# Attention, soft mixture and a tanh layer on one core: moving M's steps, two joins, one square and the linear part's last steps

## The chip, the cores and the metric

The kernel runs on one core of one Trainium2 chip. The metric is the device time of one execution in microseconds (us); the profile shows one execution as a hardware profiler recorded it. The engines in it are TensorE (PE for matmuls, PEld for weight loads), VectorE (DVE), ScalarE (ACT), GpSimd (POOL) and the queue that issues the DMAs (SP).

## What is computed

Three layers follow one another on 3072 tokens of 512 numbers. The first two (a linear attention with decay, then a mixture of experts with soft routing) end about halfway through the span and the change does not touch them. The third is where the change lies:

```python
def _moe2_ref(x, w_in, w_out):          # x 3072x512, w_in 512x2048, w_out 2048x512
    h = x @ w_in
    g = h - np.tanh(h)
    return (g @ w_out).astype(np.float32)
```

The input x of this layer is itself a product of a 3072x32 gate c and a 32x512 table (the mixture's output, `so` in the kernel), so h = c (so w_in). The kernel never forms x: it builds M = so w_in (32x2048) and works on c M.

## The kernel before

**Chunks.** The third layer is a walk over 96 chunks, numbered n = 0 to 95. A chunk is one of six column groups of 512 tokens (c) with one of sixteen blocks of 128 hidden columns (f). `TURNS` lists the order as (c, first f, last f): (0,0-2), (1,0-2), (2,0-2), (3,0-4), (4,0-8), (5,0-12), and then the remaining blocks of each c. So chunks 0 and 1 belong to c 0, 2 and 3 to c 1, 4 and 5 to c 2, 6 to 9 to c 3, 10 to 17 to c 4, 18 to 29 to c 5, 30 to 39 to c 0, 40 to 53 to c 1, and so on.

**What a chunk does.** `d_of(n)` is one matmul into one of three PSUM banks taken in turn (L805), so the matmul of chunk n has to wait until chunk n-3 has been read. `s_of(n)` squares it on ACT (L809); for the chunks in `POOL_R` ACT also writes a copy e with a bias (L812). `r_of(n)` multiplies the two into r, on DVE (L823), or on GpSimd for the chunks in `POOL_R` = 13, 16, 21, 26, 29, 34, 37 (L821). `r` is called the rest below. `product` is the second matmul (L830), four per chunk, one for each quarter of the 512 tokens, into four PSUM banks that a stretch of one c shares. When a stretch ends, `keep` copies the four sums to SBUF (ACT, L836, in the first stretch of a c) or adds them to what is there (DVE, L838).

**The loop.** In step n of the loop the program issues d and s of chunk n+3 (`ahead`), the rest of chunk n+2, then decoding steps, then products of chunk n. In the last two chunks of a stretch the products of both are issued together at the last one, eight in a row. Last, `run(n)` issues what was put down for step n with `at(n, ...)`. The order in each engine's queue is the order of the program; it is written out by hand (`manual_schedule`), and each engine works through its own queue in order. The first chunk whose index is in `LATE` (8) has its d and s issued after the products of step 5 and ahead of that step's copies of sums.

**Decoding.** w_in and w_out come as 64-bit floats and are loaded raw in slabs wi0 to wi7 and wo0 to wo7. A slab is decoded in two halves, each a cast on GpSimd (`cast`, L117) followed by a join on DVE (`join`, L121), which takes two operands from SBUF. `DECODE_AT` names the step in which a slab's last join is issued; `LEAD` spreads the four operations over the steps k-3, k-2 (casts), k-1 and k (joins). The last join of a slab frees its buffer and lets SP load another slab. A decoded wo slab is rounded for the products by `round_wo`, the first half on ACT (L788), the second on GpSimd (L790).

**M.** Two wi slabs give a quarter m of M (four blocks f). `make_m` multiplies (L753) and copies the result to SBUF (L758); `turn_m` turns it (L778) and DVE copies the bias columns `mt` (L781); `put_m` spreads it (L765), ACT writes `ms` (L769) and DVE subtracts a remainder into 32 rows of it (L770). All d of the blocks of quarter m need that last instruction. For m 1 and 2 and 3 the three parts come 2, 3 and 4 steps behind the second slab's decoding (`DUE`); for the second half of quarter 0 they come in the steps `HALF` = 2, 3, 4. They share one PSUM bank (`MISC`), so each part waits for the copy out of the part before.

**The linear part.** A correction qc (128x512) is built late (`LINEAR` = 43, 47): `linear_2` multiplies in steps 43 to 46, `linear_3` in step 47 makes qr in PSUM (L891) and then qc: rows 0 to 63 by an ACT copy (L893), a rounded copy qh of the other rows by ACT (L894), and four DVE operations on 32 rows each in steps 48 to 51 (L897 to L902). The first four products with qc (L1066) stand in step 53, each behind the products of one token quarter.

Of the kernel before, what the change touches and what calls it, by code (L numbers as in the profile page):

```python
# [9 lines left out]
F32 = mybir.dt.float32  # L10
# [48 lines left out]
DECODE_AT = [0, 2, 4, 6, 10, 12, 14, 17, 21, 24, 26, 30, 33, 36]  # L59
LEAD = 3, 2, 1, 0  # L60
DUE = 2, 3, 4, 1
HALF = 2, 3, 4
LATE = 8,
LINEAR = 43, 47
CHECK = 57, 59, 63
# [7 lines left out]
def tile_main(ctx, tc, qkv, lam, phi, w1, w2, w_in, w_out, out):  # L73
# [501 lines left out]
    with pool("exp") as ep:  # L575
# [136 lines left out]
        def now(ops):  # L712
            for f in ops:
                f()
# [42 lines left out]
        rows = slice(js[0] * NS, (js[-1] + 1) * NS)  # L757
        (nc.vector.tensor_copy if half == 1 else nc.scalar.copy)(m_t[m][rows], mp_[rows])  # L758

    def put_m(m, half=None, bk=None):  # L760
        pp = bank(bk or MISC, [P, 4, P], "pp")
        js = range(4) if half is None else range(2 * half, 2 * half + 2)
        rows = slice(js[0] * NS, (js[-1] + 1) * NS)
        for j in js:
            nc.tensor.matmul(  # L765
                pp[:, j], put[rows, j], m_t[m][rows], start=True, stop=True, skip_group_check=True)
        pp = pp[:, js[0]:js[-1] + 1].rearrange("p j f -> p (j f)")
        sl = slice(m * 512 + js[0] * P, m * 512 + (js[-1] + 1) * P)
        nc.scalar.activation(out=ms[:, sl], in_=pp, func=AF.Copy)  # L769
        nc.vector.tensor_tensor(  # L770
            out=ms[64:96, sl], in0=pp[64:96], in1=ms[64:96, sl].bitcast(F32), op=ALU.subtract)
        placed.update(2 * m + j // 2 for j in js)

    def turn_m(m, half=None, bk=None):
        js = range(4) if half is None else range(2 * half, 2 * half + 2)
# [113 lines left out]
    def linear_3(qs):  # L889
        qr = bank(MISC, [P, DM], "qr")  # L890
        nc.tensor.matmul(qr, gsum, qs, start=True, stop=True)  # L891
        qh = lt_all[:, :DM]
        nc.scalar.activation(out=qc[:64], in_=qr[:64], func=AF.Copy)  # L893
        nc.scalar.activation(out=qh[64:].bitcast(F32R), in_=qr[64:], func=AF.Copy)  # L894
        ql = tmp("e", bufs=2)
        return [
            lambda: nc.vector.tensor_tensor(out=ql[96:], in0=qr[96:], in1=qh[96:], op=ALU.subtract),  # L897
            lambda: nc.vector.tensor_scalar(
                out=ql[96:], in0=ql[96:], scalar1=ends[96:, 1:2], scalar2=0.0, op0=ALU.mult, op1=ALU.add),
            lambda: nc.vector.scalar_tensor_tensor(  # L900
                out=qc[96:], in0=qh[96:], scalar=ends[96:, 0:1], in1=ql[96:], op0=ALU.mult, op1=ALU.add),
            lambda: nc.vector.tensor_tensor(  # L902
                out=qc[64:96], in0=qr[64:96], in1=qh[64:96], op=ALU.subtract),
        ]


# [65 lines left out]
        return z  # L972

    LA = 3
    due = {}

    def at(n, f):
        due.setdefault(n, []).append(f)

    def run(n):  # L980
        for f in due.pop(n, []):
            f()

# [18 lines left out]
    early[0]()  # L1002
    round_wo(0, 1)
    r_of(1)
    now(early[1:])

    def decoded(n, w, i):
        if w == "wi" and i == 1:
            at(HALF[0], lambda: make_m(0, 1))
            at(HALF[1], lambda: turn_m(0, 1))  # L1010
            at(HALF[2], lambda: put_m(0, 1))
        elif w == "wi" and i % 2:
            at(n + DUE[0], lambda: make_m(i // 2))
            at(n + DUE[1], lambda: turn_m(i // 2))
            at(n + DUE[2], lambda: put_m(i // 2))
            if i == NF // 2 - 1:
                at(LINEAR[0] - 3, linear_0)
                at(LINEAR[0] - 3, linear_1)
                at(LINEAR[0] - 2, linear_g)
                at(LINEAR[0] - 1, lambda: state.update(gt=linear_gt()))  # L1020
        elif w == "wo":
            for h in range(2):
                at(n + DUE[3] + h, lambda h=h: round_wo(i, h))
            if i == NF // 2 - 1:
                for j in range(4):
                    at(LINEAR[0] + j, lambda j=j: linear_2(state["gt"], j))
                at(LINEAR[1], lambda: state.update(linear=linear_3(state["qs"])))
                for j in range(4):
                    at(LINEAR[1] + 1 + j, lambda j=j: state["linear"][j]())
                at(CHECK[0], check_1)  # L1030
                at(CHECK[1], check_2)
                at(CHECK[2], lambda: state.update(flag=check_3()))

    for n in range(NN):
# [4 lines left out]
            ahead()  # L1039
        if n + LA - 1 < NN:  # L1040
            r_of(n + LA - 1)
        for slab, k in zip(parts, DECODE_AT):
            for h, lead in enumerate(LEAD):
                if k - lead == n and k:
                    parts[slab][h]()
            if k == n:
                decoded(n, *slab)
# [9 lines left out]
                product(*s, n, f == lo, False)  # L1057
        if last:

            for s in ops:  # L1060
                if hi - lo > 1 and n > 1:
                    product(*s, n - 1, f - 1 == lo, False)
                product(*s, n, f == lo, hi < NF)
                if hi == NF:
                    op, t, sl = s
                    nc.tensor.matmul(op, c4[:, c, t * P:(t + 1) * P], qc[:, sl], start=False, stop=True)  # L1066
            if n + LA in LATE:
                ahead()
            for s in ops:
                keep(c, *s, lo, hi)  # L1070
        run(n)
    assert not due, sorted(due)
    scheduled.close()


# [82 lines left out]
```

## Time and profile before

| | us |
|---|---|
| median of three runs | 311.65 (311.45 to 311.79) |
| the profiled execution's own time | 311.51 |
| its span, first to last instruction | 309.6 |

| engine | busy us | share of the span |
|---|---|---|
| PE | 294.8 | 95% |
| DVE | 181.3 | 59% |
| ACT | 134.3 | 43% |
| POOL | 115.2 | 37% |

TensorE was granted its full clock nearly throughout (mean 0.995). The third layer begins at about 155 us of the span. In the views below a row of the timeline gives start, duration, engine, line, operation, output and inputs, shapes, count, and in brackets how long the engine sat idle before it and what released it. A duration includes any time in which the instruction had begun and was held up inside the engine. Several instructions that follow one another directly are merged into one row with their count. The d matmuls of L805 stand in the order of the chunks, so the number of a chunk is found by counting them.

### The profile page before, as it was taken

How to read it: one execution, taken by the hardware profiler on the slowest of the kernel's cores; microseconds unless marked ns; L12 is line 12 of the kernel's file. 1: busy time of each engine (PE TensorE's matmuls, PEld its weight loads, DVE VectorE, ACT ScalarE, POOL GpSimd, SP SyncE). 2: the span in 40 equal slices, each digit the busy share in tenths (PEclk: the TensorE clock that was granted, in tenths of full speed). 3: DMA queues.
4: the chain of work that ended last, by engine and by line, in shares of the span. 5: the costliest groups of instructions: out<-in, count | busy, mean ns of one | idle time of the engine just before them, and what ended most of it. 6: DMA issues, size and time to landing. Idle time of an engine off the chain costs nothing.

```text
span 309.6 us, 7420 instructions
## 1 busy us (share of the span) xinstructions
PE 294.8 (95%) x2996; PEld 213.6 (69%) x2996; DVE 181.3 (59%) x330; ACT 134.3 (43%) x280; POOL 115.2 (37%) x167
## 2 busy tenths in 40 slices
PE   8999999999999999999989889999999899999992
PEld 7788787878878774445466567777655677787771
DVE  4844455544654244520269667696872877968783
ACT  1433343344333433232248669586633554454420
POOL 6366566765653104112276445686600001000000
PEclk9999999999999999999999999999999999999997
DMA  6999999999999999999988747562000030303154
GB/s 209 386 402 395 396 399 394 395 399 398 392 403 396 383 362 344 389 393 396 391 308 318 268 142 285 194 230 110 0 2 0 2 135 0 135 2 135 70 202 143
DMA packets 32679, 79.77 MB, mean 258 GB/s; under 512 B 3008, under 2 KB 3328, under 8 KB 32640
## 3 DMA queue, kind: packets, MB, share of 16 engines
q1 hardware_dynamic: 32512, 79.18, 68.5%
q8 instruction: 25, 0.41, 0.5%
q14 instruction: 14, 0.11, 0.1%
q0 software_dynamic: 128, 0.07, 0.1%
HBM read 72.94 MB, written 6.29 MB: 256 GB/s over the span
## 4 chain that ended last, share of the span: by engine, by line
PE 80%; DVE 8%; issue 4%; DMA 3%; ACT 2%; POOL 1%; DVEq 0%; ACTq 0%; POOLq 0%
PE ops L830 22%; PE sc L286 7%; PE xp L310 7%; PE dps L805 6%; PE op L610 5%; PE hp L586 5%; PE xnp L344 4%; PE xp L303 4%; DVE r L823 3%; PE up L319 3%; DMA qk<-in_qkv 3%; DVE part L838 2%; PE ltp L333 2%; PE ap L388 2%; PE wp L419 2%
## 5 line engine op out<-in xcount | busy, mean ns | idle before, releaser
L830 PE MATMUL ops<-wr,r 128*128 128x512 f32 (+1 forms) x388 | 109.0, 397 | 1.2 <-ACT part L836 0.9
L830 PEld LDWEIGHTS ops<-wr,r 128*128 128x128 f32 x388 | 72.3, 188 | 22.2 <-ACT part L836 3.1
L809 ACT ACTIVATE s<-dps 128x512 f32<-128x512 f32 x96 | 56.9, 603 | 54.1 <-PE dps L805 52.8
L823 DVE SCALAR_TENSOR_TENSOR r<-dps,mt,s 128x512 fp32r<-128x512 f32 x89 | 64.8, 746 | 20.2 <-ACT s L809 19.4
L805 PE MATMUL dps<-c,ms 128*128 128x512 f32 x96 | 39.5, 425 | 4.2 <-DVE r L823 2.3
L290 DVE TENSOR_TENSOR at<-sc,dtab 128x512 f32<-128x512 f32 x48 | 30.8, 683 | 15.1 <-PE sc L286 15.1
L265 POOL TENSOR_TENSOR kc<-k,dtab 128x512 f32<-128x512 f32 x20 | 21.2, 1058 | 26.6 <-PE up L319 23.6
L258 POOL TENSOR_TENSOR qs<-qk,ql 128x512 f32<-128x512 f32 x20 | 25.5, 1275 | 14.6 <-DMA qk<-in_qkv 14.5
L346 ACT COPY xn<-xnp 128x512 f32<-128x512 f32 x24 | 14.0, 585 | 38.9 <-PE xnp L344 38.9
L286 PE MATMUL sc<-qk 64*128 64x128 f32 x384 | 27.9, 285 | 1.4 <-DMA qk<-in_qkv 1.4
L805 PEld LDWEIGHTS dps<-c,ms 128*128 128x128 f32 x96 | 17.9, 188 | 15.6 <-DVE r L823 7.8
L310 PE MATMUL xp<-at,v 128*64 128x128 f32 x384 | 26.3, 279 | 0.0
L286 PEld LDWEIGHTS sc<-qk 64*128 64x128 f32 x384 | 23.3, 187 | 4.2 <-issue 1.9
L313 ACT COPY xt<-xp 128x256 f32<-128x256 f32 x48 | 17.9, 372 | 16.9 <-PE xp L310 16.4
L310 PEld LDWEIGHTS xp<-at,v 128*64 128x64 f32 x384 | 20.5, 136 | 4.1 <-issue 3.9
L325 DVE TENSOR_TENSOR st<-up,sd 128x256 f32<-128x256 f32 x16 | 6.8, 425 | 23.4 <-PE up L319 22.0
L117 POOL CAST top<-wi 128x512 f16<-128x512 bf16 x16 | 14.3, 907 | 13.7 <-DMA wi<-in_w_in 13.1
L838 DVE TENSOR_TENSOR part<-ops,part 128x512 f32<-128x512 f32 (+1 forms) x29 | 17.9, 665 | 0.9 <-PE ops L1066 0.9
L610 PE MATMUL op<-w,hz 128*32 128x512 f32 x128 | 16.5, 594 | 0.0
L117 POOL CAST top<-wo 128x512 f16<-128x512 bf16 x16 | 15.2, 978 | 2.3 <-DMA wo<-in_w_out 2.1
L121 DVE SCALAR_TENSOR_TENSOR wif<-wi,top 128x512 uint32<-128x512 uint32 x16 | 13.3, 842 | 4.2 <-POOL top L117 4.2
L344 PE MATMUL xnp<-cst,xt 128*128 128x128 f32 x96 | 15.7, 287 | 0.0
(185 smaller groups left out, 344.3 us busy)
## 6 DMA issues: line engine op xcount, KB each, us to landing
w<-in_w SPq DMA_DIRECT2D x64, 512.0 KB, 8.4
qk<-in_qkv SPq DMA_DIRECT2D x24, 512.0 KB, 8.4
wi<-in_w_in SPq DMA_DIRECT2D x16, 512.0 KB, 4.0
wo<-in_w_out SPq DMA_DIRECT2D x16, 512.0 KB, 4.2
v<-in_qkv SPq DMA_DIRECT2D x24, 256.0 KB, 8.5
out<-part SPq DMA_DIRECT2D x23, 256.0 KB, 2.2
k<-in_qkv SPq DMA_DIRECT2D x14, 256.0 KB, 8.0
out<-part SPq DMA_DIRECT2D x2, 128.0 KB, 3.5
```

Source lines behind the costliest of these rows:

```text
L117: nc.gpsimd.tensor_copy(out=every(top().bitcast(F16), 2, 1)[:, sl], in_=every(raw().bitcast(BF16)[:, 4:], 4, 0)[:, sl])
L258: nc.gpsimd.tensor_tensor(out=qs_t[u], in0=qk_t[u][:, 0], in1=ql, op=ALU.mult)
L286: nc.tensor.matmul(sc[h2][:, p], qk[sl, 1, p], qk[sl, 0, p], start=True, stop=True)
L290: nc.vector.tensor_tensor(out=by_head(at_t[u], h2), in0=sc[h2], in1=by_head(dtab, h2), op=ALU.mult)
L310: nc.tensor.matmul(at_head(p, h2), v[:, h * DH:(h + 1) * DH], at[:, h], start=c == 0 and p < 2, stop=True, skip_group_check=True)
L344: nc.tensor.transpose(xnp[:, p], xt[:, p // 2, p % 2], ident)
L610: nc.tensor.matmul(op[g * NS:(g + 1) * NS], hz_t[e % 3][:, q], w2_t[e, q // 4][:, g], start=e == 0 and q < 4, stop=e == NE - 1 and q >= 4, ...
L805: nc.tensor.matmul(d_t[n], ms[:, f * P:(f + 1) * P], c4[:, c], start=True, stop=True)
L809: nc.scalar.activation(out=s, in_=d_t[n], func=AF.Square, scale=math.sqrt(1.0 / 3))
L823: nc.vector.scalar_tensor_tensor(out=r_t[n], in0=d, scalar=mt[:, f, NS:], in1=s, op0=ALU.add, op1=ALU.mult)
L830: nc.tensor.matmul(op, r_t[n][:, t * P:(t + 1) * P], wr_t[f // 2][:, f % 2, sl], start=first, stop=last)
L838: nc.vector.tensor_tensor(out=pt, in0=op, in1=pt, op=ALU.add)
```

## The change

Eight things are moved or rewritten; the arithmetic is the same.

1. Joins of wi1 (two halves): they stood in front of the loop behind the rest of chunk 1; now the first stands behind the rest of chunk 2 (step 0) and the second behind the rest of chunk 3 (step 1).
2. The second half of M's quarter 0: `make_m(0, 1)` goes from the end of step 2 to the middle of step 3's eight products; `turn` and `put` stay in the steps 3 and 4.
3. The square of chunk 8 is issued behind the four copies of sums of step 5 (its d stays ahead of them).
4. Quarter 1 of M: make, turn and put go from the ends of the steps 8, 9, 10 to the end of 7, the middle of 9 and the end of 9; ACT's and DVE's parts of the put are split in two pieces of 256 columns.
5. Quarter 2: from steps 19, 20, 21 to 18, 19, 20.
6. Quarter 3: steps as before (32, 33, 34), but ACT's and DVE's part of the put is issued in step 35, behind the rest of chunk 37.
7. The linear part: in step 48 ACT copies 64 rows of qr to SBUF and GpSimd does five operations on 32 rows each; DVE's four are gone. ACT's copy to rows 0 to 63 of qc goes behind that, to step 49.
8. Helpers (`at_mid`, `at_r`) for work that is issued in the middle of a step's products or right behind its rest.

```diff
-HALF = 2, 3, 4
+HALF = 3, 3, 4
+SECOND = 7, 9, 9
+THIRD = 18, 19, 20
@@ def put_m(m, half=None, bk=None, pieces=1, later=None)
-        nc.scalar.activation(out=ms[:, sl], in_=pp, func=AF.Copy)
-        nc.vector.tensor_tensor(
-            out=ms[64:96, sl], in0=pp[64:96], in1=ms[64:96, sl].bitcast(F32), op=ALU.subtract)
+        def take(i):
+            src = pp[:, js[0] * P + i * n:js[0] * P + (i + 1) * n]
+            sl = slice(m * 512 + js[0] * P + i * n, m * 512 + js[0] * P + (i + 1) * n)
+            nc.scalar.activation(out=ms[:, sl], in_=src, func=AF.Copy)
+            return lambda: nc.vector.tensor_tensor(
+                out=ms[64:96, sl], in0=src[64:96], in1=ms[64:96, sl].bitcast(F32), op=ALU.subtract)
+        def place():
+            for rest in [take(i) for i in range(pieces)]:
+                rest()
+        if later is None:
+            place()
+        else:
+            at_r(later, place)
@@ def linear_3(qs)
-        nc.scalar.activation(out=qc[:64], in_=qr[:64], func=AF.Copy)
+        qf, ql = tmp("e", bufs=2), tmp("e", bufs=2)
+        tt = lambda out, in0, in1, op: nc.gpsimd.tensor_tensor(out=out, in0=in0, in1=in1, op=op)
+        end = lambda i: ends[96:, i:i + 1].to_broadcast([32, DM])
         nc.scalar.activation(out=qh[64:].bitcast(F32R), in_=qr[64:], func=AF.Copy)
+        def rest():
+            tt(qc[64:96], qf[64:96], qh[64:96], ALU.subtract)
+            tt(ql[96:], qf[96:], qh[96:], ALU.subtract)
+            tt(ql[96:], ql[96:], end(1), ALU.mult)
+            tt(qf[96:], qh[96:], end(0), ALU.mult)
+            tt(qc[96:], qf[96:], ql[96:], ALU.add)
         return [
-...
+            lambda: (nc.scalar.copy(qf[64:], qr[64:]), rest()),
+            lambda: nc.scalar.activation(out=qc[:64], in_=qr[:64], func=AF.Copy),
         ]
@@ main loop
-    now(early[1:])
+    cast_1, join_0, join_1, *early = early[1:]
+    now([cast_1] + early)
+    at_r(0, join_0)
+    at_r(1, join_1)
-            at(HALF[0], lambda: make_m(0, 1))
+            at_mid(HALF[0], lambda: make_m(0, 1))
+        elif w == "wi" and i == 3:
+            at(SECOND[0], lambda: make_m(1))
+            at_mid(SECOND[1], lambda: turn_m(1))
+            at(SECOND[2], lambda: put_m(1, pieces=2))
+        elif w == "wi" and i == 5:
+            at(THIRD[0], lambda: make_m(2))
+            at(THIRD[1], lambda: turn_m(2))
+            at(THIRD[2], lambda: put_m(2))
-            at(n + DUE[2], lambda: put_m(i // 2))
+            at(n + DUE[2], lambda: put_m(i // 2, later=n + DUE[2] + 1))
-                for j in range(4):
+                for j in range(2):
                     at(LINEAR[1] + 1 + j, lambda j=j: state["linear"][j]())
+        run(n, due_r)
-            for s in ops:
+            for i, s in enumerate(ops):
+                if i == 2:
+                    run(n, due_mid)
             if n + LA in LATE:
-                ahead()
+                d_of(n + LA)
             for s in ops:
                 keep(c, *s, lo, hi)
+            if n + LA in LATE:
+                s_of(n + LA)
```

## Rows read from the trace of the kernel before

**Rows 1.** PE's waits, 155 to 310 us: waiter, releaser, us in total, times, longest.
```profile
PE dps L805 <- DVE ms L770: 1.7, 2, 1.4
```
**Rows 2.** The chain that ended last: start, us, what.
```profile
189.57 1.91 PE ops L830 x7
...
250.32 0.93 PE ops L830 x4
```
**Rows 3.** Timeline, square of chunk 8, copies of step 5, products of chunk 6.
```profile
171.24 0.60 ACT L809 ACTIVATE s<-dps 128x512 f32<-128x512 f32 x1 [1.79 <-PE dps L805]
171.73 2.05 ACT L836 COPY part<-ops 128x512 f32<-128x512 f32 x4
...
172.36 1.97 PE L830 MATMUL ops<-wr,r 128*128 128x512 f32 x4 [0.93 <-ACT part L836]
```
**Rows 4.** Timeline, joins of wi1, d of chunk 5, DVE's copy in make_m(0, 1).
```profile
160.82 2.11 DVE L121 SCALAR_TENSOR_TENSOR wif<-wi,top 128x512 uint32<-128x512 uint32 x2
...
163.65 0.50 PE L805 MATMUL dps<-c,ms 128*128 128x512 f32 x1 [0.74 <-DVE r L823]
...
166.14 0.29 DVE L758 COPY lt_all<-mp__2509 64x128 f32<-64x128 f32 x1
```
**Rows 5.** Timeline, d of chunk 13, its e, d of chunk 14.
```profile
179.03 0.48 PE L805 MATMUL dps<-c,ms 128*128 128x512 f32 x1
...
180.09 0.74 ACT L812 ACTIVATE e<-dps,mt 128x512 f32<-128x512 f32 x1
...
182.74 0.50 PE L805 MATMUL dps<-c,ms 128*128 128x512 f32 x1 [1.41 <-DVE ms L770]
```
**Rows 6.** Timeline of POOL, rests of chunks 13 and 16, casts of wi4, rounding of wo3.
```profile
180.91 1.26 POOL L821 TENSOR_TENSOR r<-e,s 128x512 fp32r<-128x512 f32 x1 [6.02 <-ACT e L812]
182.12 1.92 POOL L117 CAST top<-wi 128x512 f16<-128x512 bf16 x2
...
186.92 1.35 POOL L821 TENSOR_TENSOR r<-e,s 128x512 fp32r<-128x512 f32 x1 [2.35 <-ACT e L812]
...
188.90 0.62 POOL L790 CAST wr<-wf 128x512 fp32r<-128x512 f32 x1
```
**Rows 7.** Timeline, joins that meet GpSimd's work.
```profile
201.27 2.39 DVE L121 SCALAR_TENSOR_TENSOR wf<-wo,top 128x512 uint32<-128x512 uint32 x2
...
201.81 1.30 POOL L821 TENSOR_TENSOR r<-e,s 128x512 fp32r<-128x512 f32 x1 [2.74 <-issue]
...
204.22 0.60 POOL L790 CAST wr<-wf 128x512 fp32r<-128x512 f32 x1
204.24 1.12 DVE L121 SCALAR_TENSOR_TENSOR wif<-wi,top 128x512 uint32<-128x512 uint32 x1
```
**Rows 8.** Timeline, d of chunk 38, put_m(3) on ACT and DVE, d of chunk 42.
```profile
216.93 0.48 PE L805 MATMUL dps<-c,ms 128*128 128x512 f32 x1
217.22 0.60 ACT L769 ACTIVATE ms<-pp 128x512 fp32r<-128x512 f32 x1 [0.58 <-PE pp L765]
...
217.85 0.69 DVE L770 TENSOR_TENSOR ms<-pp,ms 32x512 fp32r<-32x512 f32 x1 [1.73 <-ACT ms L769]
...
221.36 0.50 PE L805 MATMUL dps<-c,ms 128*128 128x512 f32 x1 [0.45 <-DVE r L823]
```
**Rows 9.** Timeline, linear part: qh, d of chunk 56, first product with qc, d of chunk 58.
```profile
240.01 0.59 ACT L894 ACTIVATE lt_all<-qr 64x512 fp32r<-64x512 f32 x1
...
245.04 0.50 PE L805 MATMUL dps<-c,ms 128*128 128x512 f32 x1 [0.79 <-DVE r L823]
...
245.85 0.47 PE L1066 MATMUL ops<-qc,c 128*128 128x512 f32 x1
...
249.93 0.39 PE L805 MATMUL dps<-c,ms 128*128 128x512 f32 x1
```
**Rows 10.** Groups of POOL instructions by form: count, busy us, mean ns, idle before.
```profile
L258 POOL TENSOR_TENSOR qs<-qk,ql 128x512 f32<-128x512 f32 x20 | 25.5, 1275 | 14.6 <-DMA qk<-in_qkv 14.5
L265 POOL TENSOR_TENSOR kc<-k,dtab 128x512 f32<-128x512 f32 x20 | 21.2, 1058 | 26.6 <-PE up L319 23.6 <-ACT k L253 2.7 <-POOL qs L258 0.3
...
L635 POOL COPY put<-cst 32x96 f32<-32x96 f32 x4 | 1.0, 256 | 0.0
```

More of the change, by code (lines that the diff above doesn't have):

```diff
@@ L758, in make_m, with put_m @@
         (nc.vector.tensor_copy if half == 1 else nc.scalar.copy)(m_t[m][rows], mp_[rows])
-    def put_m(m, half=None, bk=None):
+    def put_m(m, half=None, bk=None, pieces=1, later=None):
         pp = bank(bk or MISC, [P, 4, P], "pp")
@@ L766, in put_m @@
                 pp[:, j], put[rows, j], m_t[m][rows], start=True, stop=True, skip_group_check=True)
-        pp = pp[:, js[0]:js[-1] + 1].rearrange("p j f -> p (j f)")
-        sl = slice(m * 512 + js[0] * P, m * 512 + (js[-1] + 1) * P)
-        nc.scalar.activation(out=ms[:, sl], in_=pp, func=AF.Copy)
-        nc.vector.tensor_tensor(
-            out=ms[64:96, sl], in0=pp[64:96], in1=ms[64:96, sl].bitcast(F32), op=ALU.subtract)
-        placed.update(2 * m + j // 2 for j in js)
+        pp = pp.rearrange("p j f -> p (j f)")
+        n = len(js) * P // pieces
+        def take(i):
[7 more added lines that the diff above has]
+                rest()
+            placed.update(2 * m + j // 2 for j in js)
+        if later is None:
+            place()
+        else:
+            at_r(later, place)
     def turn_m(m, half=None, bk=None):
@@ L892, in linear_3 @@
         qh = lt_all[:, :DM]
-        nc.scalar.activation(out=qc[:64], in_=qr[:64], func=AF.Copy)
+        qf, ql = tmp("e", bufs=2), tmp("e", bufs=2)
+        tt = lambda out, in0, in1, op: nc.gpsimd.tensor_tensor(out=out, in0=in0, in1=in1, op=op)
+        end = lambda i: ends[96:, i:i + 1].to_broadcast([32, DM])
         nc.scalar.activation(out=qh[64:].bitcast(F32R), in_=qr[64:], func=AF.Copy)
-        ql = tmp("e", bufs=2)
-        return [
[L897 to L903, printed above, removed]
+        def rest():
[4 more added lines that the diff above has]
+            tt(qc[96:], qf[96:], ql[96:], ALU.add)
+        return [
+            lambda: (nc.scalar.copy(qf[64:], qr[64:]), rest()),
+            lambda: nc.scalar.activation(out=qc[:64], in_=qr[:64], func=AF.Copy),
         ]
@@ L974, in tile_main, with at_mid, at_r, run @@
     LA = 3
-    due = {}
+    due, due_mid, due_r = {}, {}, {}
     def at(n, f):
         due.setdefault(n, []).append(f)
-    def run(n):
+    def at_mid(n, f):
+        due_mid.setdefault(n, []).append(f)
+    def at_r(n, f):
+        due_r.setdefault(n, []).append(f)
+    def run(n, due=due):
         for f in due.pop(n, []):
@@ L1067, in tile_main @@
             if n + LA in LATE:
-                ahead()
+                d_of(n + LA)
             for s in ops:
                 keep(c, *s, lo, hi)
+            if n + LA in LATE:
+                s_of(n + LA)
         run(n)
-    assert not due, sorted(due)
+    assert not due and not due_mid and not due_r
     scheduled.close()
```

## The prediction

> **What bounds the kernel now.** I read the waits of PE first, then the chain that ended last, then the timeline around each place that the diff touches. All of them lie in the third layer, 155 to 310 us. PE is the bound there: a product takes 0.233 us (four in 0.93, [rows 2]), a chunk has five matmuls, and in most steps the next chunk starts 1.16 us after the last. So only the places where PE stands still count. The ones near the change are these. The d of chunk 5 waits 0.74 us for a rest that stands behind two joins [rows 4]. The products of chunk 6 wait 0.93 us for copies of sums [rows 3] and are then spread over 1.97 us. The d of chunk 14 waits 1.41 of the 1.7 us that PE loses to `ms` [rows 1, 5]; the other wait, that of chunk 26, is 0.25. At 189.57 a product waits for GpSimd's rounding of wo3, which ends at 189.52 [rows 2, 6]. The d of chunk 42 waits 0.45 us for DVE [rows 8], that of chunk 56 0.79 us [rows 9]. These sum to under 5 us, so no part of the change can bring much more, and each must be followed to what is late next.
>
> **The joins and M's quarter 0 (1, 2).** With the joins behind the rests of chunks 2 and 3, the d of chunk 5 no longer waits: 0.74 us off. But DVE's work up to its copy for make_m(0, 1) is the same, and DVE runs without a gap from 160.82 on. Before, that copy stands at 166.14 [rows 4]; now the rest of chunk 5 and a join of wi2 (0.7 and 0.9) stand ahead of it, so it ends at about 167.9 and turn_m, next on PE, waits for it. Before, turn ran at 167.4. The products of chunks 4 and 5 follow at 169.0 against 168.9. Gain of both: 0 (from -0.3 to 0.2).
>
> **The square behind the copies (3).** The square of chunk 8 begins at 171.24 because its d comes after eight products; the four copies queued behind it begin at 171.73, one each 0.49 us ((2.05-0.60)/3), and the products of chunk 6 keep that pace until 174.33 [rows 3]. Without the square the first copy can begin when its sum is whole, two products after 169.0, at 169.6, and the fourth at about 171.0. Chunk 6 then starts behind the d of chunk 9 at 171.4 and is done at 172.4: 1.9 us sooner. The square itself is 0.3 us later and so is the second join of wi3, which make_m(1) needs; at about 173.5 that costs PE 0.1. Gain 1.9 (1.5 to 2.1).
>
> **Quarter 1 a chunk sooner (4).** Make (1.0 us), turn (0.25) and put (0.9) now all stand ahead of the d of chunk 13. In sum PE reaches the d of chunk 14 with `ms` already written: 1.41 us more, so about 3.3 us at that point, 179.4 against 182.74. But chunk 13 gains only 0.9: its d goes from 179.03 to 178.1, since put and its wait on DVE's copy of mt stand ahead of it, and on ACT its square and its e stand behind the four copies of step 9 and the two pieces of the put. Its e then ends at 179.75 against 180.83 [rows 5].
>
> **What is late next: GpSimd.** That e releases GpSimd's queue: rest 13 (1.26), two casts of wi4 (1.92), rounding of wo2 (0.61), rest 16 (1.35), cast of wi5 (0.7), rounding of wo3 (0.62) [rows 6]. Before, GpSimd also sat idle 2.35 us in it, waiting for chunk 16's e, and the rounding that PE needs ended 8.6 us after rest 13 began. Now PE comes sooner and that idle time goes. Five joins of DVE (wo2's second, two of wo3, two of wi4) then fall between. [rows 7] show what a join costs that meets GpSimd: two joins took 2.39 us, the second ending 0.55 after the rest that began at 201.81 and took 1.30; a join at 204.24 took 1.12, ending 0.54 after the rounding of 204.22. So the two do not overlap: whichever began first is finished, the other then needs about 0.54. Without any meeting GpSimd's chain is 6.0 to 6.5 us, and the product that waits would come at about 186; with five joins in between (5 x 0.54 = 2.7) it is 8.5 to 8.9, and comes at 179.8 + 8.5 = 188.3 (rest 17 on DVE, which also needs those joins, comes at 187 to 188.7). The joins are queued back to back in just this stretch, so I take the serial value. Of 3.3 us, **1.2** are left at 189.57 (0.7 to 3.0). That is the gain of parts 1 to 4.
>
> **Quarter 2 (5).** The 0.25 us at chunk 26 goes. But DVE works without a gap from the instruction after that to about 212 us, and its copy of mt and its part of the put now stand ahead of rests 22 and 23, so it enters that stretch no sooner; PE then waits longer for rest 28 at 206. Gain 0 (-0.3 to 0.4).
>
> **Quarter 3 later (6).** On DVE the order does not change: rest 36, the subtraction, the first join of wo7, rest 38. DVE already sits idle 1.73 us in front of that subtraction, waiting for ACT [rows 8]. ACT's write of `ms` now goes behind a rounding of wo6 and the square of chunk 38, whose d ends at 217.41: square 217.43, write 217.92 to 218.52, subtraction at 218.55 against 217.85. So DVE is 0.70 later, and behind it without a gap stand two joins, rests 38 to 41 and four additions of sums, for which PE already waits at chunk 42 [rows 8] and again for the sums. Nothing covers it: **0.7 lost** (0 to 0.8).
>
> **Linear part (7).** ACT: qh 239.4 to 240.0 (0.59, [rows 9]), square of chunk 51, then the copy of qr, done at 241.1. DVE's four operations (0.70, 0.48, 0.75, 0.69) leave its queue, so rest 53 and the d of chunk 56 come without a wait: PE reaches the first product with qc at 244.8 instead of 245.85 [rows 9]. GpSimd needs five operations for qc. No row shows one on 32 partitions of 512; with 128 partitions, two operands cost 1.275 and one operand repeated 1.058 [rows 10]. That fewer partitions do not help is suggested by L635 (32x96 in 0.256, with 0.268 for L913's 128x96). So 3 x 1.275 + 2 x 1.058 = 5.94, and qc is whole at 247.1: PE stands still 2.3 us. From there to the d of chunk 58 are 15 matmuls, 3.5 us: 250.6 against 249.93 [rows 9], **0.7 lost**. The upper bound is five of 1.35 (rest 16, [rows 6]): 6.75, 1.5 lost. The lower is a cost that falls with the partitions: then qc is there before PE, and 1.7 us of waits of before (0.79, and DVE's lag behind it) go. DVE is free, but it wasn't what PE would wait for.
>
> The Trainium skill speaks against this part: GPSIMD Engine Reference, § 4.1 Engine selection, wants elementwise work on a tile on VectorE, since GpSimd is about twice as slow with two inputs. § 3.1 measures 4497 ns for 2048 columns; a quarter of it is 1.12 us as an estimate, five of them 5.6, and the loss would be 0.35 instead of 0.7. The rows agree on the direction (1.275 against DVE's 0.69 to 0.75).
>
> **Sum.** 1.2 + 0 - 0.7 - 0.7 = 0.2 lost on the profiled execution's 311.51, whose span is 309.6 with 1.9 around it; nothing outside the span changes. The median is 311.65, so I forecast **311.8**.
>
> **Rivals.** (a) Slower: the five GpSimd operations hold the first product with qc longer than I take. From 6.4 us on (1.28 each, or a start 0.5 later) the sum is over 0.6 lost; at 6.9 the product comes at 248.0, 1.6 lost instead of 0.7, and the time is 312.7. For it: the operations depend on one another, and nothing covers PE there. Against: rows of 1.06 for repeated operands. (b) Faster: joins and GpSimd's work meet less often than I let them, so that 2.6 of the 3.3 us survive: 310.3. For it: in the stretch of before, GpSimd's idle 2.35 us let the joins through; DVE may find other gaps. (c) Faster: GpSimd's operations on 32 partitions cost about what half the columns cost, 0.6 each, so qc is ready at 244.2 and 1.7 is gained, not 0.7 lost: 309.4. Against: L635. (d) Part 6 does not do what its place says, because DVE's first join of wo7 hides the later subtraction: 0.7 less, 311.1. Against: the join stands behind it in the queue.
>
> **Chances.** About 0.2% (0.6 us) is what a measurement of this kernel can tell from no change. Forecast 0.42, (a) 0.29, (b) 0.16, (c) 0.08, (d) 0.05. Faster by over 0.2%: (b) and (c), 0.24. Within: forecast and (d), 0.47. Slower: (a), 0.29. The range goes from a little under (b) to (a): 309.9 to 312.8, leaving out (c) and the far ends.
>
> **What would show it.** In the profile of the changed kernel: the four copies of step 5 begin before the square of chunk 8, and chunk 6's products end near 172.4 (part 3). The d of chunk 14 begins near 179.4 without a wait for DVE (part 4). The rounding of wo3 ends about 1.3 us sooner than 189.52, joins among GpSimd's rests last 1.1 us or more, and PE stands still at the products of chunks 16 and 17 (the chain). ACT's write of M's quarter 3 stands behind the square of chunk 38, DVE's subtraction 0.7 later against the d of chunk 38 (part 6). The first product with qc waits over 2 us for POOL (part 7). I am wrong if GpSimd's five operations take under 4 us, if the rounding of wo3 ends more than 2 us sooner, or if DVE catches up the 0.7 us before the sums of chunk 39.

## The result and the profile after

| | before | after |
|---|---|---|
| median, same comparison, us | 311.45 | 314.50 |
| ratio, 95% interval | | 1.0066 (1.0040 to 1.0092) |
| the profiled execution's own time, us | 311.51 | 314.61 |
| its span, us | 309.6 | 312.8 |
| PE busy, us | 294.8 | 296.8 |
| POOL busy, us | 115.2 | 122.5 |

The change makes the kernel slower, by 0.7% in the ratio of the comparison and by 1.0% in the two medians; 0.2 us, under 0.1%, was forecast, and the time lies above the range. The times of after spread from 312.35 to 316.23 us (disturbed executions, here 317.25 and 317.75, in e4 316.23 and in f1 314.32, are left out of spreads, means and ratios). They follow roughly the mean granted clock of each execution: 0.996 at 312.35, 0.994 at 312.67, 0.992 at 314.61, 0.986 at 315.57. That points at TensorE's clock before any line is read.

To find the place I divide the third layer at four instructions that all kernels have: M0 is the first matmul of the first `make_m`, and d14, d38, d44, d58 are the starts of the first matmuls of these chunks. All rows of this table come from the timeline of one profiled execution of each kernel. "e" to "h" are the experiments below. "Fall" says that the granted clock drops in that stretch from full speed to about half.

| kernel | M0 to d14 | d14 to d38 | d38 to d44 | d44 to d58 |
|---|---|---|---|---|
| before | 27.48 | 34.19 | 8.47 | 24.53 |
| after | 24.96 | 36.74 | 9.19 | 27.21, fall |
| e1, part 7 undone | 24.84 | 36.77 | 9.18 | 24.54 |
| e2, after with the wait filled | 25.97, fall | 36.74 | 9.19 | 25.79 |
| e3, parts 1 to 5 | 26.29, fall | 36.75 | 8.47 | 24.54 |
| e4, e3 with rests on DVE | 25.28 | 35.40 | 8.46 | 24.52 |
| f1, after with `linear_2` packed | 27.88, long fall | 36.74 | 9.20 | 22.78 |
| f2, parts 1 and 2 | 27.96 | 34.22 | 8.48 | 24.53 |
| f3, parts 3 to 5, rests on DVE | 24.56 | 35.47 | 8.46 | 24.54 |
| f4, f3 with packed part 7 | 24.39 | 35.47 | 8.47 | 22.79 |
| g1, after again | 23.88 | 36.78 | 9.19 | 25.78 |
| g2, e2 again | 26.32, fall | 36.75 | 9.20 | 25.79 |
| g3, part 7 alone | 27.46 | 34.22 | 8.47 | 27.32, fall |
| g4, before with rests on DVE | 27.43 | 34.15 | 8.46 | 24.52 |
| h1, after without parts 1, 2 | 24.76 | 36.75 | 9.18 | 27.22, fall |
| h2, h1 with the wait filled | 24.75 | 36.76 | 9.18 | 25.79 |
| h3, part 7 alone again | 27.41 | 34.19 | 8.48 | 27.20, fall |
| h4, part 7 alone, wait filled | 27.43 | 34.22 | 8.47 | 25.81 |

The first two rows carry the result: 2.52 us less to d14, 2.55 more to d38, then 0.72 and 2.68 more, 3.43 in all. The profiled executions differ by 3.10; the layers before and the end of the third account for the remaining 0.3.

**Where PE waits now.** PE's waits in the third layer of after: waiter, releaser, us in total, times, longest.
```profile
PE dps L820 <- DVE r L838: 3.7, 8, 1.1
PE ops L1108 <- POOL qc L909: 2.5, 1, 2.5
PE tp L793 <- DVE lt_all L760: 1.0, 1, 1.0
```
The wait for `ms` of [rows 1] is gone. In its place stand a wait for qc of 2.5 us, one of 1.0 behind DVE's copy in `make_m(0, 1)`, and more waits of a d for a rest on DVE.

**What became of the gain at d14.** Timeline of after: start, us, engine, line, operation, out and in, count, and in brackets the idle time before it and its releaser.
```profile
167.33 0.29 DVE L760 COPY lt_all<-mp__2521 64x128 f32<-64x128 f32 x1
167.67 0.43 PE L793 MATMUL tp<-tsel,lt_all 64*128 64x66 f32 x2 [1.01 <-DVE lt_all L760]
169.87 2.05 ACT L851 COPY part<-ops 128x512 f32<-128x512 f32 x4 [0.28 <-PE ops L845]
171.54 1.09 PE L845 MATMUL ops<-wr,r 128*128 128x512 f32 x4
171.78 1.77 ACT L824 ACTIVATE s<-dps 128x512 f32<-128x512 f32 x3
...
178.55 0.48 PE L820 MATMUL dps<-c,ms 128*128 128x512 f32 x1
180.00 0.51 PE L820 MATMUL dps<-c,ms 128*128 128x512 f32 x1
180.63 1.29 POOL L836 TENSOR_TENSOR r<-e,s 128x512 fp32r<-128x512 f32 x1 [5.56 <-ACT e L827]
180.98 2.62 DVE L123 SCALAR_TENSOR_TENSOR wf<-wo,top 128x512 uint32<-128x512 uint32 x2
181.88 2.35 POOL L119 CAST top<-wi 128x512 f16<-128x512 bf16 x2
184.18 1.11 DVE L123 SCALAR_TENSOR_TENSOR wf<-wo,top 128x512 uint32<-128x512 uint32 x1
184.32 0.50 PE L820 MATMUL dps<-c,ms 128*128 128x512 f32 x1 [0.55 <-DVE r L838]
184.72 1.71 POOL L836 TENSOR_TENSOR r<-e,s 128x512 fp32r<-128x512 f32 x1
185.88 2.22 DVE L123 SCALAR_TENSOR_TENSOR wif<-wi,top 128x512 uint32<-128x512 uint32 x2
186.01 0.50 PE L820 MATMUL dps<-c,ms 128*128 128x512 f32 x1 [0.25 <-DVE r L838]
187.52 1.05 POOL L805 CAST wr<-wf 128x512 fp32r<-128x512 f32 x1
188.02 1.40 DVE L838 SCALAR_TENSOR_TENSOR r<-dps,mt,s 128x512 fp32r<-128x512 f32 x2
188.82 0.50 PE L820 MATMUL dps<-c,ms 128*128 128x512 f32 x1 [1.14 <-DVE r L838]
```
The copies of sums stand ahead of the square of chunk 8 and chunk 6's products are done at 172.63, against 174.33 in [rows 3]. The d of chunk 14 comes at 180.00 with no wait, 1.45 us behind that of chunk 13, where it was 3.71 in [rows 5]. By the d of chunk 20 hardly any of the gain is left (188.82; before, the d's of the chunks 19 and 20 follow one another from 188.66 on): PE waits for rests at the d of the chunks 17, 18 and 20, 0.55, 0.25 and 1.14 us. The joins on DVE and GpSimd's work run into each other: two joins take 2.62 us, one 1.11, two 2.22, where one alone takes 0.68, and GpSimd's two casts take 2.35 instead of 1.92 [rows 6]. The rest of chunk 17 on DVE begins only at 188.02 and the d of chunk 20 waits 1.14 for it. The chain that ended last, in the same stretch (start, us, what), is DVE alone. "Issue" is time in which an engine waited for nothing that the profile shows; here it falls into the last of the joins above, which was held. From 180.31 to 188.02 DVE is never idle waiting for a cast of GpSimd, so it is not the length of GpSimd's queue as such that holds it up.
```profile
183.52 0.74 DVE r L838
184.26 1.03 DVE wf L123
185.29 0.66 DVE r L838
185.96 1.32 DVE wif L123 x2
187.27 0.75 issue
188.02 0.75 DVE r L838
...
188.82 0.50 PE dps L820
```

**M's quarter 3 and the linear part.** Timeline of after around the d of chunk 38, then around the first product with qc.
```profile
216.74 0.48 PE L820 MATMUL dps<-c,ms 128*128 128x512 f32 x1
217.75 0.59 ACT L775 ACTIVATE ms<-pp 128x512 fp32r<-128x512 f32 x1
218.37 0.69 DVE L776 TENSOR_TENSOR ms<-pp,ms 32x512 fp32r<-32x512 f32 x1 [2.45 <-PE dps L820]
221.88 0.50 PE L820 MATMUL dps<-c,ms 128*128 128x512 f32 x1 [0.77 <-DVE r L838]
...
241.82 1.29 POOL L909 TENSOR_TENSOR qc<-e,lt_all 32x512 fp32r<-32x512 f32 x1 [17.57 <-ACT e L921]
243.18 1.30 POOL L909 TENSOR_TENSOR e<-e,lt_all 32x512 f32<-32x512 f32 x1
244.56 1.04 POOL L909 TENSOR_TENSOR e<-e,ends 32x512 f32<-32x512 f32 x1
245.56 1.04 POOL L909 TENSOR_TENSOR e<-lt_all,ends 32x512 f32<-32x512 f32 x1
246.68 1.26 POOL L909 TENSOR_TENSOR qc<-e 32x512 fp32r<-32x512 f32 x1
247.99 0.50 PE L1108 MATMUL ops<-qc,c 128*128 128x512 f32 x1 [2.52 <-POOL qc L909]
```
DVE's subtraction stands 1.63 us behind its d, against 0.92 in [rows 8]: 0.71 later. The five operations on 32 partitions take 5.93 us, and PE stands 2.52. What follows the stand is seen in the windows of after (stretch, us, busy time and count of PE, PEld, DVE, ACT, POOL, granted clock, DMA share, GB/s):
```profile
249.00:250.00 1.00, 1.00 (x5) 0.79 (x4) 0.92 (x2) 0.00 (x0) 0.00 (x0) 0.77 0.00 0
250.00:251.00 1.00, 1.00 (x4) 0.81 (x3) 0.69 (x1) 0.00 (x0) 0.00 (x0) 0.50 0.89 332
251.00:252.00 1.00, 1.00 (x4) 0.71 (x4) 0.62 (x2) 0.19 (x1) 0.00 (x0) 0.50 0.85 313
252.00:253.00 1.00, 1.00 (x4) 0.81 (x3) 1.00 (x3) 0.40 (x1) 0.00 (x0) 0.52 0.43 162
253.00:254.00 1.00, 1.00 (x6) 0.82 (x5) 0.39 (x1) 0.43 (x1) 0.00 (x0) 1.00 0.64 242
```
PE is busy all the time, yet does four matmuls in a us instead of six: the granted clock went from 1.00 to 0.50 (2.4 to 1.2 GHz) for about 3 us. The prediction has no term for that.

### The profile page after: what moved, and what is told of

It reads as the page before. It is cut to its first block, busy times and chain, and to the rows that moved or that the text cites. A ratio compares the mean times of both kernels' runs of the same rounds, so it can differ in the third digit from the quotient of the medians.

```text
span 312.8 us, 7429 instructions
## 1 busy us (share of the span) xinstructions
PE 296.8 (95%) x2996; PEld 215.2 (69%) x2996; DVE 181.7 (58%) x327; ACT 135.3 (43%) x282; POOL 122.5 (39%) x172
## 4 chain that ended last, share of the span: by engine, by line
PE 76%; DVE 10%; DMA 5%; issue 3%; POOL 2%; ACT 2%; SPq 1%; DVEq 0%; ACTq 0%
PE ops L845 21%; PE sc L288 8%; PE xp L312 7%; PE dps L820 6%; PE op L612 5%; DVE r L838 4%; PE hp L588 4%; PE xnp L346 4%; PE xp L305 4%; PE up L321 3%; DMA w<-in_w 2%; DMA qk<-in_qkv 2%; PE ops L1108 2%; DVE wf L123 2%; PE ltp L335 2%
## 5 line engine op out<-in xcount | busy, mean ns | idle before, releaser
L845 PEld LDWEIGHTS ops<-wr,r 128*128 128x128 f32 x388 | 73.1, 190 | 19.1 <-DVE part L853 2.2
L119 POOL CAST top<-wi 128x512 f16<-128x512 bf16 x16 | 15.5, 981 | 15.0 <-DMA wi<-in_w_in 14.0
L123 DVE SCALAR_TENSOR_TENSOR wif<-wi,top 128x512 uint32<-128x512 uint32 x16 | 14.0, 877 | 4.9 <-POOL top L119 4.9
L588 PE MATMUL hp<-w,si 128*32 128x256 f32 x256 | 15.5, 382 | 0.0
```

The lines of the kernel that those rows point to most:

```text
L588: nc.tensor.matmul(hp[j * NS:(j + 1) * NS], si[:, k], w[:, k % 2, j * 256:(j + 1) * 256], start=k == 0, stop=k == KD - 1, skip_group_check ...
L845: nc.tensor.matmul(op, r_t[n][:, t * P:(t + 1) * P], wr_t[f // 2][:, f % 2, sl], start=first, stop=last)
```

## The experiments

Two readings are to be tested. First, the gain of parts 3 and 4 is lost because joins and GpSimd's work exclude each other; the rival is that DVE's own work in this stretch is simply too much. Second, part 7 costs its wait and, because of that wait, a stretch at the lower clock; the rival is that the clock falls for another reason, such as the DMA traffic that begins there.

**e1: part 7 undone.** `linear_3` and its four operations on DVE as before.
```diff
...
-                for j in range(2):
+                for j in range(4):
                     at(LINEAR[1] + 1 + j, lambda j=j: state["linear"][j]())
```


> The changed kernel with its last steps of the linear part back on DVE (part 7 undone), all else as changed. Theory A (the wait for GpSimd's five operations and the half clock behind it make the loss): about 2.6 us faster than the changed kernel, 0.5 slower than before (312.0), mean granted clock back at 0.995, and runs within 1 us of one another. Rival B (the loss comes from the moved steps of M and the joins): stays near 314, with a spread of several us.

Median 313.04, ratio to before 1.0029 (1.0005 to 1.0053). The last stretch is back at 24.54, before's value; the other three are those of after. So part 7 costs 2.67 in the profile, and what is left, 0.66 by stages, is part 6's 0.71 less 0.05. The median fell by less, 1.46, and the times spread from 310.97 to 314.07, where 312.0 and runs within 1 us were expected. Six of the twelve executions have a mean granted clock of 0.991 or 0.992 (0.997 in the profiled one), so the clock seems to fall in e1 too; where, no profile of e1 shows.

**e2: after, with the wait filled.** In step 53, ahead of the first product with qc, nine matmuls whose result is not used.
```diff
+                    if n == 53 and i == 0:
+                        wp = bank(MISC, [P, DM], "wp")
+                        for _ in range(9):
+                            nc.tensor.matmul(wp, c4[:, 0, :P], c4[:, 0], start=True, stop=True)
```


> The changed kernel with nine matmuls (9 x 0.233 = 2.1 us) into a free PSUM bank ahead of the first product with qc, in the time that PE stands still there; their result is not used. Theory A1 (the granted clock falls because PE stood still, and that costs 1.6 us on top of the 2.5 us wait): granted clock 1.00 from 249 to 253, time about 312.9, spread gone. Rival A2 (the wait alone costs, what follows it is late for DVE's sums and SP's transfers): 314.5 as the changed kernel, or more.

Median 313.46, ratio 1.0064 (1.0037 to 1.0092). The last stretch takes 25.79 with no fall, 1.42 less than after, although qc comes no sooner. But in this profile the clock fell elsewhere, near 170 us, and took 1.0 of it back. The ratio does not move; the two stretches do. The clock behind the wait came out as expected, the spread did not go: the times reach from 312.37 to 316.70.

**e3: parts 1 to 5.** e1, and quarter 3 placed as before.
```diff
-            at(n + DUE[2], lambda: put_m(i // 2, later=n + DUE[2] + 1))
+            at(n + DUE[2], lambda: put_m(i // 2))
```


> Before with parts 1 to 5 alone (joins, square, M's quarters 0 to 2); quarter 3 and the linear part as before. Theory C (what they gain by chunk 14, some 2.5 us, is given back by chunk 20 because joins and GpSimd's work exclude one another): 311.4, within 0.3 of before; d of chunk 14 near 180, d of chunk 21 near 191. And it should be 0.7 under the kernel with only the linear part undone, if the later subtraction of quarter 3 costs what its rows say; if that step is free, both are equal.

Median 312.21, ratio 1.0007 (0.9984 to 1.0029). The stretch from d38 to d44 is back at 8.47: part 6 costs 0.71 to 0.72, and nothing hides it. This profile too has a fall near 170, behind a wait of `turn_m`. A row of its timeline, then windows:
```profile
167.63 0.43 PE L793 MATMUL tp<-tsel,lt_all 64*128 64x66 f32 x2 [1.01 <-DVE lt_all L760]
```
```profile
170.00:171.00 1.00, 1.00 (x4) 0.81 (x3) 0.97 (x3) 0.84 (x2) 1.00 (x3) 0.50 0.93 324
171.00:172.00 1.00, 1.00 (x3) 0.76 (x3) 0.95 (x1) 0.73 (x2) 0.60 (x2) 0.50 1.01 393
172.00:173.00 1.00, 1.00 (x4) 0.75 (x3) 0.00 (x0) 0.73 (x3) 0.62 (x1) 0.50 1.00 377
```

**e4: e3 with the rests of chunks 13 and 16 on DVE,** which takes two of the operations that meet the joins out of GpSimd's queue.
```diff
-POOL_R = 13, 16, 21, 26, 29, 34, 37
+POOL_R = 21, 26, 29, 34, 37
```


> Parts 1 to 5 alone, and the rests of chunks 13 and 16 on DVE instead of GpSimd. Theory C (DVE's joins wait for GpSimd's rests, 1.3 us each): two rests of 0.67 more on DVE, but two joins of 1.7 us become 0.7 and GpSimd's queue loses 2.6 us: rest 17 comes about 1 us sooner and the time is 310.3 to 310.8. Rival D (DVE has too much to do in that stretch, whatever GpSimd does): 1.3 us more work, 312.5.

Median 310.49, ratio 0.9952 (0.9927 to 0.9977): faster than before. d14 to d38 takes 35.40 instead of 36.75. DVE now has two more rests and is done sooner all the same. Its timeline in e4:
```profile
181.73 0.68 DVE L123 SCALAR_TENSOR_TENSOR wf<-wo,top 128x512 uint32<-128x512 uint32 x1
182.33 0.74 DVE L838 SCALAR_TENSOR_TENSOR r<-dps,mt,s 128x512 fp32r<-128x512 f32 x1
182.99 0.75 DVE L123 SCALAR_TENSOR_TENSOR wf<-wo,top 128x512 uint32<-128x512 uint32 x1
...
185.59 0.67 DVE L123 SCALAR_TENSOR_TENSOR wif<-wi,top 128x512 uint32<-128x512 uint32 x1
```
Joins of 0.67 to 0.75, with rests between them, where after has 1.1 to 1.3 each. The first reading stands: with more work DVE is done sooner, which the rival does not allow.

**g4: before with the same line,** to see whether it is a gain of its own.

> Before with the rests of chunks 13 and 16 on DVE and nothing else. Theory C (those rests hold up joins only where M's quarter 1 comes a chunk sooner; in before GpSimd waits 2.4 us for chunk 16 and the joins pass in that time): 0.3 to 0.6 us under before (the wait for the rounding of wo3 goes), far from the 1.5 that parts 3 to 5 with them bring. Rival D (rests on DVE are better by themselves): 1 us or more under before.

Median 311.80, ratio 0.9997 (0.9975 to 1.0019): nothing, and all four stretches as in before. I had expected a gain; I read it so that there was none to have, since PE waits for `ms` there [rows 5]: the line only pays once d14 comes sooner.

**f2: parts 1 and 2 alone** (before with the two joins behind the rests and `HALF` = 3, 3, 4).

> Before with parts 1 and 2 alone (joins of wi1 behind rests, M's half quarter in the middle of step 3). Theory F (turn_m now stands 1 us still behind DVE's copy, and in part of the runs the clock falls to half for 3 us behind it, which costs 1.4 us): best runs as the best of before, 311.0, mean 0.4 to 1.0 slower than before, single runs at 313 to 314. Rival G (the falls near 170 us come from what parts 3 and 4 do): as before in mean and spread.

Median 312.14, ratio 1.0014 (0.9991 to 1.0036). M0 to d14 is 0.48 longer, without a fall: the wait of `turn_m` (1.01, as in after) is more than the 0.74 it replaces, which accounts for 0.27 of it. Between the theory and its rival f2 does not decide: its times (310.96 to 313.98) spread as before's do in the same comparison (310.65 to 314.08).

**f3: parts 3 to 5 with the rests on DVE** (e4 with parts 1 and 2 undone).
```diff
-HALF = 3, 3, 4
+HALF = 2, 3, 4
...
-            at_mid(HALF[0], lambda: make_m(0, 1))
+            at(HALF[0], lambda: make_m(0, 1))
```


> Parts 3 to 5 without 1 and 2, and the rests of chunks 13 and 16 on DVE. Theory F: as the kernel with parts 1 to 5 and those rests on DVE in its best runs (308.8 to 309.5), but no clock fall near 170 us, so a smaller spread and a mean 0.5 to 1.0 lower, about 309.7. Rival G: no different from that kernel, or slower by the 0.7 us that part 1 took off the wait of chunk 5.

Median 310.38, ratio 0.9956 (0.9935 to 0.9977), as e4, in runs a little closer together (309.23 to 311.21; e4's reach from 308.81 to 312.30). M0 to d14 is 24.56, 0.7 less than in e4. The mean, 310.28, is 0.16 under e4's; 0.5 to 1.0 was expected, so what parts 1 and 2 cost over many executions is not shown here.

**f1: after with `linear_2` packed.** Its four products stand in steps 43 and 44 and `linear_3` in 45, so that GpSimd begins two steps sooner.
```diff
-LINEAR = 43, 47
+LINEAR = 43, 45
-                    at(LINEAR[0] + j, lambda j=j: linear_2(state["gt"], j))
+                    at(LINEAR[0] + j // 2, lambda j=j: linear_2(state["gt"], j))
```


> The changed kernel with the four parts of linear_2 in the steps 43 and 44 instead of 43 to 46 and linear_3 in step 45 instead of 47; nothing else moved. GpSimd's five operations then begin some 2.4 us sooner against the products. Theory A (it is the wait for them that costs 2.5 us, and the half clock behind it): PE waits under 0.3 us for GpSimd, the clock stays whole from 245 to 255, and the best runs come to 310.0 (312.4 less the 2.4 us), the mean some 3 us under the changed kernel. Rival E (GpSimd's operations slow DVE or ACT, or the place of the first product with qc is not what decides): within 1 us of the changed kernel.

Median 310.99, ratio 0.9954 (0.9926 to 0.9982). The wait for qc is 0.2 instead of 2.5, and d44 to d58 takes 22.78, 1.75 less than in before. GpSimd's five operations are no longer than they were; they are off PE's path. This profile has a long fall ahead of d14 (27.88 against after's 24.96), and the median is still under before's.

**g1, g2: after and e2 once more; g3: part 7 alone.** g1 has after's code, g2 has e2's, and g3 is before with after's `linear_3` and its list of two.

> The changed kernel itself, to stand on one chip and beside the same runs of before as the three kernels sent with it. Best runs 312.4, mean about 314, 2 us over before; mean granted clock of the runs between 0.986 and 0.996, lower where the time is longer.

> The changed kernel with nine matmuls into a free bank while PE waits for qc, once more, on the same chip as the changed kernel. Theory A1 (half clock behind the wait costs 1.4 us in most runs of the changed kernel): best runs equal, mean 0.8 to 1.4 us lower than the changed kernel's. Rival A2 (the wait alone costs; the clock falls elsewhere as often): means equal within 0.3.

> Before with part 7 alone (last steps of the linear part on GpSimd). Theory A: best runs 1.0 us over the best of before (the wait of 2.5 us less the 1.5 us that DVE's four operations cost there), mean 1.5 to 2.4 over it, with the clock at half behind the wait in part of the runs. Rival B (parts 1 to 6 make the loss): within 0.5 us of before.

g1: 314.48, 1.0106 (1.0082 to 1.0129). Its profile caught an execution without a fall: wait 2.52, last stretch 25.78, the value of the filled kernels. g2: 314.50, 1.0091 (1.0074 to 1.0109), again a fall ahead of d14 (26.32) and none behind qc (25.79). The two medians are equal and the means within 0.12, as the rival says, which I had not expected of a filled wait. g3: 314.12, 1.0080 (1.0052 to 1.0107), with a last stretch of 27.32 and the others as in before: part 7 alone costs nearly as much as the whole change on the same chip (314.12 against 314.48), and its fall needs neither a sooner d14 nor parts 1 and 2. Nor does it need DMA traffic, as one of its windows shows (the last two columns are DMA share and GB/s):
```profile
248.00:249.00 1.00, 1.00 (x4) 0.79 (x3) 0.52 (x1) 0.00 (x0) 0.00 (x0) 0.50 0.00 0
```

**h1, h2: after without parts 1 and 2, as it is and filled; h3, h4: part 7 alone again, as it is and filled.** In no profile without parts 1 and 2 does the clock fall ahead of d14, so that such a fall should not blur the comparison.

> The changed kernel without parts 1 and 2. Theory F: no clock fall near 170 us, 0.3 us less in that stretch; the wait for qc and its falls remain: best runs 312.1, mean 313.3. Rival: as the changed kernel, near 314.

> The changed kernel without parts 1 and 2, and with nine matmuls into a free bank while PE waits for qc. Theory A1: no fall anywhere in the third layer, all runs near the best of the same kernel without them, mean 0.8 to 1.4 lower. Rival A2: the same mean within 0.3.

> Before with part 7 alone, beside the same with matmuls in the wait. Best runs 1.2 over the best of before without a fall, 2.6 over it with one; mean about 2.3 over.

> Before with part 7 alone and nine matmuls into a free bank while PE waits for qc. Theory A1: no fall behind the wait, mean 1.2 over before, 0.8 to 1.4 under the same kernel without them. Rival A2: the same mean within 0.3.

| | median us | ratio (95%) | d44 to d58 |
|---|---|---|---|
| h1 | 314.37 | 1.0083 (1.0055 to 1.0112) | 27.22 |
| h2, filled | 313.28 | 1.0057 (1.0042 to 1.0072) | 25.79 |
| h3 | 314.03 | 1.0067 (1.0047 to 1.0087) | 27.20 |
| h4, filled | 313.12 | 1.0055 (1.0033 to 1.0077) | 25.81 |

One window of h1, then the same of h2, after the products with qc begin:
```profile
249.00:250.00 1.00, 1.00 (x4) 0.72 (x4) 0.64 (x1) 0.00 (x0) 0.00 (x0) 0.50 0.19 72
```
```profile
249.00:250.00 1.00, 1.00 (x6) 0.83 (x5) 1.00 (x2) 0.00 (x0) 0.00 (x0) 1.00 0.20 78
```
Same place, same DMA traffic: the filled kernel keeps its clock. Over all profiles the clock falls behind the wait for qc in 4 of 5 where PE stands still (after, g3, h1, h3, not g1) and in 0 of 4 where it is filled (e2, g2, h2, h4). Each fall costs 1.4 to 1.5 in the stage table, and filling takes 1.1 and 0.9 off the medians. All executions together agree: the mean granted clock is 0.989 to 0.994 in the twelve of h1 and h3, and 0.993 to 0.999 in the eighteen of h2 and h4, but for one of 0.986 at 315.74. That standing still there sets off the fall is thus shown, and what one fall costs is measured.

What the falls cost in the mean of many executions is not. The means, which the expectations named, differ by 0.9 (h1, h2) and only 0.3 (h3, h4); the second is the rival's value. The intervals of the ratios overlap, too. In h3 one of six stays at 312.31 and the others lie at 313.8 to 314.1. Leaving out parts 1 and 2 did not bring h1 what was expected (mean 314.2 instead of 313.3).

**f4: f3 with the packed part 7,** and without part 6.

> The kernel with parts 3 to 5 and the two rests on DVE, and besides the linear part on GpSimd with linear_2 packed into two steps. Theory A: DVE's four operations gone and no wait for qc, so the 1.7 us that PE loses around chunks 56 to 58 go: about 1.6 us under that kernel, 307.5 to 308.5. Rival E: no gain or a loss from GpSimd's operations beside DVE's rests.

Median 308.50 (307.69 to 309.12), ratio 0.9891 (0.9867 to 0.9916): 1.1% faster than before and more than that against after. It has all the gains: 24.39, 35.47, 8.47, 22.79. PE's waits in the third layer of f4, of which the one for qc is now the least:
```profile
PE dps L820 <- DVE r L838: 2.6, 5, 0.8
...
PE ops L1105 <- POOL qc L909: 0.2, 1, 0.2
```

## Why the prediction was wrong

**Parts 1 and 2: nothing gained, as forecast, but a new wait.** The prediction saw that turn would wait for DVE's copy at about 167.9 (it ended at 167.62). It called the trade even. f2 shows 0.48 lost, 0.18 past the lower bound. It also lacked a fall: with parts 1 and 2 the clock falls near 170 in 4 of 9 profiles (e2, e3, g2, f1), without them in 0 of 9. So a cost of up to 3 us in some executions was not in the sum (f1 against after, 27.88 and 24.96). And it did not count that joins meet GpSimd's casts here, too: of the joins ahead of DVE's copy two took 1.14 and 1.20 in after. In g1, the same code, none of them took over 0.69, `turn_m` waited 0.44, and d14 came 1.08 sooner behind M0:
```profile
167.86 0.43 PE L793 MATMUL tp<-tsel,lt_all 64*128 64x66 f32 x2 [0.44 <-DVE lt_all L760]
```

**Part 3: right.** Chunk 6's products end at 172.63; 172.4 was forecast.

**Part 4: mechanism right, what is left of it wrong.** From M0 the d of chunk 14 came 2.52 us sooner; 3.3 was forecast. The step that failed is "of 3.3 us, 1.2 are left at 189.57": nothing is left, 61.70 us from M0 to d38 against 61.67 before. (Its sum is off as well: 6.0 to 6.5 plus 2.7 is 8.7 to 9.2, not 8.5 to 8.9, and with 8.7 about 1.0 would be left.) Its two halves:

- Chunk 13's d came 0.26 sooner (23.51 behind M0 against 23.77), where the step had 0.9. This figure varies: 0.38 in e1 and 1.34 in g1, whose joins ahead of `turn_m` were not held. All the rest of d14's gain is the shorter way from d13 to d14 (1.45 for 3.71), and by d38 that brings nothing: GpSimd's queue is released by chunk 13's e, not by d14. From d13 to d38 before takes 37.90 and after 38.19; e1, g1, h1 and h2, with M0 to d14 between 23.88 and 24.84, take 38.20 to 38.23. The stretch goes with d13, whenever that comes; in g1 1.0 of the gain is thus left at d38 (60.66 behind M0).
- The meetings of joins and GpSimd's work were to make the rounding of wo3 end 8.5 us behind that e. It ended at 188.57, 8.02 behind it (180.55). But what bound was the rest of chunk 17 on DVE, which the prediction named only in brackets, at 187 to 188.7: it began at 188.02, and the d of chunk 20 had to wait. PE stood still at the d's of the chunks 17, 18 and 20 (1.94 us together), not at products as the prediction had it. The chain of waits runs through DVE's queue, where five joins took 5.95 (2.62 + 1.11 + 2.22) instead of 5 x 0.68 = 3.40.

With two rests moved (e4, f3), d13 to d38 takes 36.85 and 36.92: 1.3 less than in after and 1.0 less than in before.

The joins that end about 0.54 behind a GpSimd operation [rows 7] look like a lock, not like shared bandwidth. The Trainium skill says so: SBUF — State Buffer, section "Who interferes with whom", states that a DVE instruction with two SBUF inputs contends with a GpSimd instruction that reads SBUF, and calls the contention for the ports that they share an exclusive lock. The runs agree: 0.68 alone, 1.1 to 1.3 when they meet, and 1.3 us of the layer's time for it.

**Part 5: not tried alone.** Its wait for `ms` is gone, as forecast, and parts 3 to 5 together bring nothing by d38 beyond d13's gain (h1: 38.20 from d13 to d38).

**Part 6: right.** 0.7 forecast, 0.71 measured (e1 against e3). Rival (d) falls.

**Part 7: mechanism right, both terms short.** The five operations took 5.93; 5.94 was forecast. That fewer partitions do not help, taken from two small rows, is shown: 1.29 and 1.04 with 32 partitions against 1.275 and 1.058 with 128 [rows 10]. The stand was 2.52, 2.3 forecast. But "0.7 lost" came out at 1.25 without a fall (25.78 against 24.53). Counted from d44, the first product with qc begins at 22.06 where the forecast had 21.7 (247.1 less before's 225.40): GpSimd starts 0.2 later, and the gaps between its operations add 0.2. From there to d58 it is 3.72 in g1, not 3.5. Two rows of g1's timeline:
```profile
248.11 0.50 PE L1108 MATMUL ops<-qc,c 128*128 128x512 f32 x1 [2.52 <-POOL qc L909]
...
251.83 0.39 PE L820 MATMUL dps<-c,ms 128*128 128x512 f32 x1
```

**The missing step.** A stand of 2.5 us is not over when the engine starts again: the clock fell to 0.50 behind it and took another 1.43 (27.21 less 25.78). No term of the sum, no bound and no rival had that. Added to the forecast it alone gives 313.2, above the range. But the other two terms suffice as well: without the fall the stages of after still lose 2.0, and h2, whose profile has none, has a median of 313.28. Rival (a) named the place and the direction, at 312.7; with the fall it would have been 314.1, close to the measured time by luck, since (a) keeps the 1.2 of part 4.

The Trainium skill has the rule that I did not weigh: TensorE: Matmul & The Clock Gate, section "Why this matters for your kernels", advises against long gaps between bursts of matmuls, since throughput drops after them. The runs show such a drop behind 4 of 5 stands of 2.5 us, and a fall also followed 4 of 8 waits of `turn_m` of 0.95 to 1.33 us.

**In one sum,** from the stage table of after: parts 1 to 5 gain 0.0 where 1.2 was forecast; part 6 loses 0.7 as forecast; part 7 loses 1.25 plus 1.43 where 0.7 was forecast. That makes 3.4 lost instead of 0.2.

What stays open: why one execution falls and the next does not (after and g1 have the same code), and whether the falls near 170 are set off by `turn_m`'s wait itself or by what stands close to it. Filling that wait was not tried, and a wait of 0.93 at the products of chunk 6 is followed by no fall in any of the six profiles that have it (before, f2, g3, g4, h3, h4).

## What to carry to other kernels

Price a new wait on TensorE twice: the stand, and the stretch after it at the lower clock; here it was 1.4 us behind a wait of 2.5, in 4 of 5 profiles, and filling or shortening the wait took it off. When an earlier stage lets the queues behind it come sooner, count the pairs of instructions that then overlap on DVE and GpSimd; here moving two operations from GpSimd to the busier engine was what kept 1.3 us of the gain. Work that a slower engine takes over must start sooner by what it takes longer: the same five operations cost 2.7 us behind step 47 and, with the steps ahead of them packed, gained 1.75 behind step 45.

## What the hardware showed that I had not expected

- The granted clock went from 1.00 to 0.50 behind single waits of PE of 2.5 us (4 of 5 profiles) and, in kernels with parts 1 and 2, 0.8 to 2.2 us behind waits of `turn_m` of 0.95 to 1.33 us (4 of 8; whether because of them is open), and came back after some 3 us of work, in f1 after nearly 7; the same code did it in one execution and not in another.
- During such a stretch the busy share of PE is 1.00. Only the count of matmuls in a us (four instead of six) and the granted clock show it.
- GpSimd takes as long for 32 partitions of 512 as for 128 (1.29 against 1.275, 1.04 against 1.058).
- Two more operations on DVE (0.74 each) shortened the stretch by 1.3 us, with joins of 0.67 to 0.75 us each in place of 1.1 to 1.3.
